# Placing the work between attention and the late expert tiles with a list scheduler instead of fixed steps

## The chip, the cores and the metric

The kernel runs on one core of a Trainium2 chip. A core has five engines with one instruction queue each, taken in order: PE (TensorE, matrix products), ACT (ScalarE), DVE (VectorE), POOL (GpSimd) and SP (SyncE, which here only starts DMA transfers). Engines wait for each other through semaphores; an instruction that waits holds up all that stands behind it on its engine. The metric is the time of one execution on the device in microseconds (us).

## What is computed

Decaying causal attention over 8 batches, 8 heads, 576 positions and head size 64, and behind it a mixture of 8 experts (512 to 1024 to 512) whose choice is sticky: a token keeps its predecessor's expert where its local gate is 0.5 or more.

```python
    scores = scale * np.matmul(q, k.transpose(0, 1, 3, 2))
    ...
    scores = np.where(causal, -1000000000.0, scores + decay)
    ...
    return np.matmul(attn, v).astype(np.float32)
...
    for b in range(B):
        prev_e = -1
        for s in range(S):
            fresh_e = int(np.argmax(logits[b, s]))
            if s == 0 or local_gate[b, s] < 0.5:
                e = fresh_e
            else:
                e = prev_e if prev_e >= 0 else fresh_e
            prev_e = e
            ...
            h = np.maximum(x[b, s] @ w1[e], 0.0)
            out[b, s] = p[e] * (h @ w2[e])
```

The 4608 tokens are x, the attention's output; logits and local gate are products of x with w_gate and w_local.

## The kernel before

Products of float32 values run as three float16 products (high by high, high by low, low by high), so each tensor is split into a high part (names that end in h) and a low part (names in l).

**Order of the phases.** Attention runs batch by batch. Routing (which token goes to which expert, in which place) follows in four groups of two batches, behind attention; the last group can only be routed when attention has ended. By then the first six batches are routed, and the first three tiles of 128 tokens of experts 0 and 1 come from them alone. These *early tiles* are computed right behind attention (L1703, L1725), and the last group's routing is done beside them. Then come the *late tiles* of expert 0 and of expert 1, then the six other experts, ranked by their number of tokens.

**One expert's early part.** `experts` (L1674) makes eight hidden tiles z of 128 columns, 12 products each (L1703, xT with wh and wl). For each, ACT writes hh (L1689) and then DVE hl (L1690), both from z in PSUM. z has two buffers, so tile n+2 waits for hl of tile n. Then three output tiles y follow, 24 products each (L1725, hh and hl with uh and ul); ACT scales y to o (L1694) and POOL scatters o to DRAM (L1695).

**Weights.** An expert's weights are eight blocks of 512 KB: four of w1 (to wh, wl) and four of w2 (to uh, ul). Each is loaded into a staging tile stg (L1857 and L1858; L1636 for the blocks split by POOL), then ACT casts the high part (L1845) and DVE makes the low part (L1849), or POOL does both (L1645, L326, L330). A staging tile comes free when its low part is made. Expert 0's w1 blocks are split by POOL during attention; its four w2 blocks, and all of expert 1's, are loaded behind attention, since expert 1's weights lie where attention's tiles were. `close_attention` gives that memory back; it stands behind the last batch's gate products (L837, from xt and xlt) and the sum that reads them (ACT half L844, DVE L848). Rank 0's weights are read ahead through the same staging tiles (`rank_loads`, L1863 and L1865).

**Routing of the last group.** `route` yields a chain over DVE, PE and ACT: maxima, `rows` (PE L1409, ACT kg L1414), a scan along 128 tokens (L1418), `ends` (PE L1422), `hold` (DVE crow L1435), `carries` (PE L1439), a second scan (L1446, copy so L1449), `back` (PE L1454), one-hot, prefix, `place` (PE L1479), slots, marks (L1505 to L1519), `invert` (PE L1525), and with it the indices (`all_idx`) by which POOL gathers the late tokens (L1671); SP transposes them (L1673). The results of a PE step share one PSUM bank, psG.

**What sets the order.** `run` (L1738) walks through the early experts' generator, which yields after every two products, and calls each piece of other work at a step number fixed in advance: AT for the gate and routing, RESTAT for the third group's probabilities, and `beside(step, ...)` for the rest. `experts` itself writes the hh and hl of a tile behind the next tile's products. An engine's instructions are thus queued in the order in which these calls come.

Of the kernel before, what the change touches and what calls it, by code (L numbers as in the profile page):

```python
# [9 lines left out]
F32 = mybir.dt.float32  # L10
# [18 lines left out]
CAP = 6  # L29
# [28 lines left out]
NP = 2  # L58
# [4 lines left out]
RESTAT = (0, 2, 8, 14, 20, 34, 35)  # L63
XG = 6
NP0 = 4
AT = (6, 15, 18, 30, 30, 36, 44, 49, 62)
# [9 lines left out]
def kernel(  # L76
# [1702 lines left out]
    for b in range(B):  # L1779
# [3 lines left out]
        for i, u in enumerate(units):  # L1783
# [85 lines left out]
    EX["NW"] = NW = []  # L1869

    def close_attention():
# [13 lines left out]
        NW.pop(0)()  # L1885
# [20 lines left out]
    def turn_xl():  # L1906
        (xl, xlt), ps = EX["xl"], bank()
        for i in range(4):
            nc.tensor.matmul(ps[:, 128 * i:128 * i + 128], lhsT=xl.rearrange("p a j d -> p (a j d)")[:, 128 * i:128 * i + 128],
                             rhs=ident16, start=(i == 0), stop=True, skip_group_check=True)  # L1910
        nc.vector.tensor_copy(flat(xlt), ps)

    crit, rest = route(B // 2 - 1, True)
    def both(*fs):
        return lambda: [whole(f) for f in fs]

    last = gate(B - 1)
# [4 lines left out]
    def beside(x, *fs):  # L1924

        at.append(x)
        todo.append(both(*fs))
# [66 lines left out]
    def half_tiles():  # L1994
# [14 lines left out]
        nc.sync.dma_start(out=T.hf[64:128], in_=T.hf[0:64])  # L2009
        NV.tensor_scalar(T.hfi, T.hf[:, 0], 2.0, T.hrow, ALU.mult, ALU.add)  # L2010
# [3 lines left out]
    def early(e, W, xT):  # L2014
        return experts(W, xT, EARLY, lambda t: EX["p"][:, CAP * e + t:CAP * e + t + 1],
                       lambda t: EX["s"][:, CAP * e + t:CAP * e + t + 1], ep, ep, 128 * EARLY, 2)
# [17 lines left out]
    def piece():  # L2034
        NW.pop(0)()
# [146 lines left out]
    for r in range(NR):  # L2182
# [99 lines left out]
```

## Time and profile before

| | us |
|---|---|
| median of 3 runs | 860.77 (857.41 to 861.67) |
| the profiled execution | 861.14 |
| its span, first to last instruction | 859.4 |
| mean granted TensorE clock | 0.963 |
| early part, first z to the first late z | 409.91 to 506.47 |

Busy time over the span: PE 91%, DVE 61%, ACT 51%, POOL 46%. The page's second part cuts the span into 40 slices of 21.5 us; a digit is the busy share in tenths. A row of the timeline gives start, duration, engine, line, operation, output and inputs, count, and in brackets the idle time before it with what ended it. PEclk is the granted clock: 1.00 is 2.4 GHz and 0.50 is 1.2 GHz.

### The profile page before, as it was taken

How to read it: one execution, taken by the hardware profiler on the slowest of the kernel's cores; microseconds unless marked ns; L12 is line 12 of the kernel's file. 1: busy time of each engine (PE TensorE's matmuls, PEld its weight loads, DVE VectorE, ACT ScalarE, POOL GpSimd, SP SyncE). 2: the span in 40 equal slices, each digit the busy share in tenths (PEclk: the TensorE clock that was granted, in tenths of full speed). 3: DMA queues.
4: the chain of work that ended last, by engine and by line, in shares of the span. 5: the costliest groups of instructions: out<-in, count | busy, mean ns of one | idle time of the engine just before them, and what ended most of it. 6: DMA issues, size and time to landing. Idle time of an engine off the chain costs nothing. (4 is left out here: it accounts for less than half of the span.)

```text
span 859.4 us, 21060 instructions
## 1 busy us (share of the span) xinstructions
PE 781.1 (91%) x8510; PEld 544.8 (63%) x8510; DVE 526.6 (61%) x1133; ACT 436.9 (51%) x811; POOL 391.3 (46%) x457
## 2 busy tenths in 40 slices
PE   5897999989999999979677899999999999999993
PEld 3675888768887788766333465674655758475541
DVE  8885888898989988987474524252470726333110
ACT  4785879678877788757222224242341414233210
POOL 9599839397948788446254013121303022120100
PEclk9897999999999999989799799999999999999997
DMA  6979949684868855477846512775372837544000
GB/s 167 180 163 186 201 97 186 136 182 116 172 153 158 175 106 110 114 142 148 214 160 162 181 37 90 182 184 174 125 215 69 211 120 185 163 139 124 26 26 22
DMA packets 196517, 122.46 MB, mean 142 GB/s; under 512 B 136220, under 2 KB 172318, under 8 KB 196396
## 3 DMA queue, kind: packets, MB, share of 16 engines
q1 hardware_dynamic: 190273, 101.68, 52.4%
q0 software_dynamic: 6144, 19.41, 7.1%
q8 instruction: 68, 1.11, 0.6%
q14 instruction: 32, 0.26, 0.1%
HBM read 72.41 MB, written 19.62 MB: 107 GB/s over the span
## 5 line engine op out<-in xcount | busy, mean ns | idle before, releaser
L1703 PE MATMUL z<-xT,wh 128*128 128x288 f16 (+4 forms) x960 | 186.2, 306 | 21.0 <-DVE hl L1690 21.0
L920 ACT ACTIVATE P<-st,nm 128x512 f32<-128x512 f32 (+3 forms) x288 | 153.0, 588 | 33.1 <-DVE nm L900 30.2
L1690 DVE SCALAR_TENSOR_TENSOR hl<-z,hh 128x576 f16<-128x576 f32 (+5 forms) x80 | 52.9, 662 | 178.6 <-ACT hh L1689 178.4
L900 DVE TENSOR_REDUCE nm<-st 128x1 f32<-128x512 f32 (+4 forms) x264 | 134.6, 544 | 17.7 <-PE st L896 13.5
L940 ACT CAST ph<-pt 128x512 f16<-128x512 f32 (+1 forms) x200 | 116.1, 584 | 46.8 <-PE pt L935 43.1
L1703 PEld LDWEIGHTS <-wh 128*128 128x128 f16 x960 | 94.0, 99 | 63.3 <-issue 21.9
L935 PE MATMUL pt<-ident,P 128*128 128x128 f32 x784 | 122.4, 280 | 6.4 <-DVE pl L944 5.6
L1695 POOL DMA_INDIRECT out_dram<-o,ranki x26 | 27.8, 1068 | 218.8 <-ACT o L1694 197.2
L1703 PE MATMUL z<-xT,wl 128*128 128x288 f16 (+4 forms) x480 | 120.5, 306 | 0.8 <-POOL wl L330 0.8
L944 DVE TENSOR_TENSOR pl<-pt,ph 128x512 f16<-128x512 f32 x168 | 111.6, 669 | 14.8 <-ACT ph L940 13.1
L1689 ACT ACTIVATE hh<-z 128x576 f16<-128x576 f32 (+5 forms) x80 | 45.9, 574 | 124.7 <-PE z L1703 124.6
L1725 PE MATMUL y<-ul,hh 128*128 128x512 f16 x288 | 109.2, 379 | 0.0
L1725 PE MATMUL y<-uh,hl 128*128 128x512 f16 x288 | 109.2, 379 | 0.0
L1725 PE MATMUL y<-uh,hh 128*128 128x512 f16 x288 | 109.2, 379 | 0.0
L935 PEld LDWEIGHTS pt<-ident,P 128*128 128x128 f32 x784 | 85.1, 143 | 23.0 <-issue 6.6
L1725 PEld LDWEIGHTS <-hh 128*128 128x128 f16 x576 | 56.2, 98 | 65.6
L914 PE MATMUL xp<-VH,pl 128*128 128x65 f16 (+1 forms) x960 | 92.1, 196 | 2.6 <-DVE pl L944 2.6
L914 PE MATMUL xp<-VH,ph 128*128 128x65 f16 (+1 forms) x960 | 93.8, 199 | 0.0
L914 PE MATMUL xp<-VL,ph 128*128 128x65 f16 (+1 forms) x960 | 92.7, 197 | 0.0
L914 PEld LDWEIGHTS <-ph 128*128 128x128 f16 (+1 forms) x1920 | 85.0, 104 | 6.4 <-issue 2.6
L889 PE MATMUL st<-KB,QB 70*128 70x256 f16 (+4 forms) x448 | 78.6, 283 | 7.5 <-DMA KB<-Ak 5.7
L889 PE MATMUL st<-Ak,Aq 128*128 128x256 f16 (+4 forms) x448 | 78.8, 286 | 4.5 <-ACT P L920 3.4
(375 smaller groups left out, 1305.7 us busy)
## 6 DMA issues: line engine op xcount, KB each, us to landing
stg<-in_moe_w_dram SPq DMA_DIRECT2D x64, 512.0 KB
xs<-xr SPq DMA_DIRECT2D x16, 512.0 KB
ldq<-in_q_dram SPq DMA_DIRECT2D x14, 512.0 KB
ldk<-in_k_dram SPq DMA_DIRECT2D x14, 512.0 KB
ldv<-in_v_dram SPq DMA_DIRECT2D x28, 256.0 KB
QB<-Aq SPq DMA_DIRECT2D x15, 256.0 KB
KB<-Ak SPq DMA_DIRECT2D x15, 256.0 KB
ldv<-in_v_dram SPq DMA_DIRECT2D x20, 64.0 KB
```

Source lines behind the costliest of these rows:

```text
L889: nc.tensor.matmul(st[p0:p0 + m, co:co + n], lhsT=queries(lq, kk, h, c), rhs=rhs, start=(ps == 0 and first and co == col), stop=(ps == 1), ...
L900: nc.vector.tensor_reduce(dst, src, axis=AX.X, op=ALU.max, negate=True)
L914: nc.tensor.matmul(xo, lhsT=a[:, c0:c0 + m], rhs=w[:, vi, :], start=False, stop=(i == n - 1 and jj == 2), skip_group_check=True)
L920: nc.scalar.activation(P[:, c0:c1].rearrange("p (k x r) -> p k r x", r=2, x=64), st[:, c0:c1].rearrange("p (k r x) -> p k r x", r=2, x=64) ...
L935: nc.tensor.matmul(U["pt"][:, i * 128:(i + 1) * 128], lhsT=P[:, i * 128:(i + 1) * 128], rhs=ident, is_transpose=True, start=(i == 0), stop ...
L940: nc.scalar.copy(U["ph"][:, :cols], U["pt"][:, :cols])
L944: nc.vector.tensor_tensor(U["pl"][:, :cols], U["pt"][:, :cols], U["ph"][:, :cols], ALU.subtract)
L1689: nc.scalar.activation(hv, z[:, 0:nh, 0:wd], AF.Relu)
L1690: nc.vector.scalar_tensor_tensor(lv, z[:, 0:nh, 0:wd], 0.0, hv, ALU.max, ALU.subtract)
L1695: nc.gpsimd.indirect_dma_start(out=outf, out_offset=bass.IndirectOffsetOnAxis(ap=scat(t), axis=0), in_=o, in_offset=None, bounds_check=NT ...
L1703: nc.tensor.matmul(z[:, a, 0:wd], lhsT=w[:, d, fc * 128:(fc + 1) * 128], rhs=xT[:, x, a * wd:(a + 1) * wd], start=(i == 0), stop=(i == len ...
L1725: nc.tensor.matmul(y, lhsT=a[:, fc, t * 128:(t + 1) * 128], rhs=u[:, fc], start=(i == 0), stop=(i == len(prods) - 1))
```

## The change

`flow` takes the place of `run` for the early part. The work is written as streams: the products of both experts, hidden high and low parts, outputs and scatters, the routing chain, the third group's probabilities, expert 0's w2 blocks, expert 1's blocks, two fetches of late tokens, the ranking, and the read-ahead for rank 0. Each step names its engine, an assumed cost, what it needs and what it gives. `flow` keeps a clock for each engine, takes the step that can start first (within 300 ns, on that engine, the stream with the lowest number), records it, and moves the clock on. It runs when the program is built, and only the order in which instructions are queued on each engine is its result. But for the drains below, the number of instructions, their sizes and the number of buffers stay as they were (SB is 3). The loads of expert 1's blocks from the third on are split off from `close_attention`, and late tokens are gathered and transposed in two streams. Besides, POOL gets a `drain` at the start of five ranked experts; in its queue each stands right behind the scatter of the expert before and ahead of the gathers for the next.

```diff
-RESTAT = (0, 2, 8, 14, 20, 34, 35)
...
-AT = (6, 15, 18, 30, 30, 36, 44, 49, 62)
+SB = 3
...
-                    stage = ctx.enter_context(tc.tile_pool(name="stage", bufs=3, side="right"))
+                    stage = ctx.enter_context(tc.tile_pool(name="stage", bufs=SB, side="right"))
...
-        NW.pop(0)()
+        NW_load.append(NW.pop(0))
...
-    def late_tok():
-        EX["x0"] = next_tokens(lambda i: EX["ga"][:, EARLY + i:EARLY + i + 1], CAP2[0] - 2 * EARLY)
...
-    todo = [turn_xl, lambda: whole(last[0]), both(*last[1:], close_attention, *crit[0:3]), both(*crit[3:6]), both(*crit[6:8]), both(*crit[8:10]),
-            both(*crit[10:13]), both(*crit[13:17]), both(*crit[17:19], all_idx, late_tok)]
-    at = list(AT)
...
-    def both_early():
-        yield from early(0, W0, EX["xT", 0])
-        yield from early(1, EX["W"], EX["xT", 1])
...
-    FW = static_weights(W0, 0, NP0, ha=HB)
-    FW.pop(0)()
-    for i in range(2 * (8 - NP0)):
-        beside(13 + 4 * i, lambda: FW.pop(0)())
-    for i in range(4 * NP):
-        beside(19 + 3 * i, lambda: EX["PW"].pop(0)())
-    REST = EX["rest"]
-    for x, f in zip(RESTAT, REST, strict=True):
-        beside(x, f)
-    beside(36, early_probs)
-    beside(19, open_ranks)
-    beside(64, lambda: EX.update(x1l=next_tokens(lambda i: EX["ga"][:, CAP + EARLY + i:CAP + EARLY + i + 1], CAP2[1] - 2 * EARLY)))
-    for i in range(16 - 2 * NP):
-        beside(65 + 24 * i // (16 - 2 * NP), piece)
-    for i, f in enumerate((totals, ranks, numbers, rank_loads, gathers, *rest, all_probs, scatters, half_tiles, caps)):
-        beside((63, 63, 64, 95, 96)[i] if i < 5 else 92 + 6 * (i - 5), f)
-    seq = sorted(range(len(at)), key=lambda x: at[x])
-    run(both_early(), [todo[x] for x in seq], [at[x] for x in seq], 400)
+    LAND = 2200
+    def flow(streams, t0):
+        clk = {x: t0 for x in ("PE", "ACT", "DVE", "POOL", "SP", "DMA")}
+        ev, lock = {}, {"owner": None, "free": (t0, "PE")}
+        heads = []
+        for prio, gen in streams:
+            heads.append([prio, gen, next(gen, None), (t0, None)])
+        while any(h[2] for h in heads):
+            able = []
+            for h in heads:
+                op = h[2]
+                if op is None or any(x not in ev for x in op.get("needs", ())):
+                    continue
+                if op.get("opens") and lock["owner"] is not None:
+                    continue
+                eng = op["eng"]
+                after = [ev[x] for x in op.get("needs", ())]
+                if op.get("seq", True) and h[3][1]:
+                    after.append(h[3])
+                if op.get("opens"):
+                    after.append(lock["free"])
+                t = max([clk.get(eng, t0), op.get("from", 0) + t0] + [e + (0 if src == eng else 200 if src != "SP" else 0) for e, src in after])
+                able.append((t, h[0], h))
+            first = min(able, key=lambda x: x[0])
+            t, _, h = min((x for x in able if x[2][2]["eng"] == first[2][2]["eng"] and x[0] <= first[0] + 300), key=lambda x: x[1])
+            op = h[2]
+            eng, cost = op["eng"], op.get("cost", 160)
+            if op.get("opens"):
+                lock["owner"] = h
+            op["fn"]()
+            if eng:
+                clk[eng] = t + cost
+            end = t + cost + op.get("lat", 0)
+            if "dma" in op:
+                clk["DMA"] = max(clk["DMA"], t + cost) + op["dma"]
+                end = clk["DMA"] + LAND
+            h[3] = (end, eng) if eng else h[3]
+            if op.get("shuts"):
+                lock.update(owner=None, free=(end, eng))
+            for x in op.get("gives", ()):
+                ev[x] = end, eng or "DVE"
+            h[2] = next(h[1], None)
...
+                    needs = [("hl", n - 2)] if c == 0 and n > 1 else []
+                    if fc == 0:
+                        needs += [("w", e, prods[c + 1][1])]
+                    yield op_("PE", 330, fn, needs, [("z", n)] if c + 2 == len(prods) else [])
...
+                    needs = [("hl", NF * e + fc)] if t == 0 else []
+                    if t == 0:
+                        needs += [("u", e, fc // 2)]
+                    if c == 0 and k > 1:
+                        needs += [("o", k - 2)]
+                    yield op_("PE", 432, fn, needs, [("y", k)] if c + 2 == len(prods) else [])
...
+            yield op_(("ACT", "DVE")[part], (500, 480)[part], fn, [("z", n)] if part == 0 else [("hh", n)], [(("hh", "hl")[part], n)])
...
+            if part == 0:
+                yield op_("ACT", 700, fn, [("y", k), "p", "closed"] + ([("sent", k - 4)] if k > 3 else []), [("o", k)])
+            else:
+                yield op_("POOL", 1000, fn, [("o", k)], [("sent", k)], lat=2500)
...
+            "slot": (("DVE", 170),) * 6, "marks": (("DVE", 640), ("DVE", 350), ("DVE", 250), ("DVE", 650), ("DVE", 760), ("DVE", 760)),
...
+        for i in range(n + half):
+            yield op_("POOL", 1050, lambda i=i: gather(i), needs, [(tag, i)], lat=2300)
+        for i in range(n + half):
+            yield op_("SP", 1300, lambda i=i: turn(i), [(tag, i)], [(tag, "t", i)], lat=2500, seq=False)
...
+    def blocks(pieces, first, ahead, give, needs=()):
+        load = lambda k: ("block", give, k)
+        yield op_("SP", 500 * ahead, pieces[0], needs, [load(k) for k in range(first, first + ahead)], dma=1600 * ahead)
+        for i in range(first, ND + NF // 2):
+            w = ("w", give, i) if i < ND else ("u", give, i - ND)
+            yield op_("ACT", 1060, pieces[1 + 2 * (i - first)], [load(i)], seq=False, gives=[("hi", give, i)])
+            more = i + ahead < ND + NF // 2
+            yield op_("DVE", 1220, pieces[2 + 2 * (i - first)], [("hi", give, i)], [w])
+            if more:
+                yield op_("SP", 0, nop, [w], [load(i + ahead)], dma=1600, seq=False)
...
+        yield op_("PE", 500, t1, opens=True, **{"from": 1000})
+        yield op_("DVE", 600, lambda: nc.vector.tensor_copy(flat(xlt), R["ps"]), shuts=True)
+        yield op_("PE", 450, last[0], opens=True, **{"from": 2800})
+        yield op_("PE", 700, last[1], **{"from": 4000})
+        yield op_("ACT", 360, last[2])
+        yield op_("DVE", 350, last[3], shuts=True)
+        yield op_(None, 0, close_attention, gives=["closed", "loads1"])
+        yield from steps_of(crit, {"marks": ["pinverted"]})
+        yield op_("DVE", 1200, all_idx, gives=["idx"])
...
+    def third():
+        yield op_("SP", 4000, rank_loads, ["numbers", ("u", 1, 3)])
...
+    def second():
+        yield op_(None, 0, nop, ["closed"])
+        PW = EX["PW"]
+        yield from by_pool(PW, 1)
+    def second_rest():
+        yield op_(None, 0, nop, ["closed", ("u", 0, 0)])
+        first = [lambda: NW_load[0]()] + list(NW)
+        yield from blocks(first, NP, ST + 3 - NP, 1)
+    FW = static_weights(W0, 0, NP0, ahead=SB, ha=HB)
+    ready = op_(None, 0, nop, gives=[("w", 0, d) for d in range(ND)])
+    e0 = CAP + EARLY
+    flow([(-9000, iter([ready])), (-3000, products()), (-6000, hidden(0)), (-6000, hidden(1)), (-4400, outputs(0)), (-4400, outputs(1)),
+          (-5600, routing()), (-5000, third_pair()), (-5500, blocks(FW, NP0, SB, 0)), (-300, second()), (-4400, second_rest()),
+          (-4400, fetch(CAP2[0] // 2 - EARLY, lambda i: EX["ga"][:, EARLY + i:EARLY + i + 1], "x0", ["idx"], bool(CAP2[0] % 2))),
+          (-4400, fetch((CAP2[1] - 2 * EARLY) // 2, lambda i: EX["ga"][:, e0 + i:e0 + i + 1], "x1l", [("x0", CAP2[0] // 2 - EARLY - 1)], bool(CAP2[1] % 2))),
+          (-3500, ranking()), (0, both_halves()), (-200, third())], clock["PE"])
...
         if r > 0:
+            todo.append(lambda: [nc.gpsimd.drain()])
+            at.append(2)
```

**ACT, right behind attention.** Names: hh is the high part of a hidden tile z of expert 0; uh from stg the cast of one w2 block of expert 0; half the gate; kg a routing step. Before:

```order
L1689 ACTIVATE hh_9640<-z_9642 128x384
L1845 ACTIVATE uh_8598<-stg_9634 128x1024
L1689 ACTIVATE hh_9640<-z_9658 128x384
L844 COPY half_9757<-psG_9704 128x36
L844 COPY half_9757<-psG_9704 64x9
L1845 ACTIVATE uh_8598<-stg_9636 128x1024
L1689 ACTIVATE hh_9640<-z_9686 128x384
L1845 ACTIVATE uh_8598<-stg_9638 128x1024
L1689 ACTIVATE hh_9640<-z_9730 128x384
```

The same place in the change:

```order
L2110 ACTIVATE hh_9687<-z_9642 128x384
L843 COPY half_9728<-psG_9669 128x36
L843 COPY half_9728<-psG_9669 64x9
L2110 ACTIVATE hh_9687<-z_9692 128x384
L2110 ACTIVATE hh_9687<-z_9742 128x384
L1844 ACTIVATE uh_8598<-stg_9636 128x1024
L1413 CAST kg_9827<-psG_9816 10x256
L2110 ACTIVATE hh_9687<-z_9795 128x384
L1844 ACTIVATE uh_8598<-stg_9638 128x1024
L1844 ACTIVATE uh_8598<-stg_9640 128x1024
L2110 ACTIVATE hh_9687<-z_9829 128x384
L2110 ACTIVATE hh_9687<-z_9872 128x384
```

The first cast of a w2 block stood between the first and the second hidden tile; now it stands behind the third, and the gate ahead of it. Three rows further on, uh from stg_9825 (expert 0's fourth w2 block) stands ahead of the last two hidden tiles.

**SP, in the middle of expert 0's early part.** Names: stg from w2 are blocks of expert 1; xT from xg are transposes of late tokens; eidi is the number of the rank 0 expert. Before, from expert 1's fifth block on:

```order
L1858 DMA stg_9794<-in_moe_w2_dram 128x2x512
L1858 DMA stg_9796<-in_moe_w2_dram 128x2x512
L1858 DMA stg_9798<-in_moe_w2_dram 128x2x512
L1673 DMA_TRANSPOSE xT_10049<-xg_10050 128x8x128
L1673 DMA_TRANSPOSE xT_10049<-xg_10053 128x8x128
L1673 DMA_TRANSPOSE xT_10067<-xg_10068 128x8x128
L1673 DMA_TRANSPOSE xT_10067<-xg_10071 128x8x128
L1673 DMA_TRANSPOSE xT_10067<-xg_10074 128x8x64
L1858 DMA stg_10088<-in_moe_w2_dram 128x2x512
L2026 TENSOR_LOAD eidi_9825
```

The same place in the change:

```order
L1857 DMA stg_9851<-in_moe_w2_dram 128x2x512
L1857 DMA stg_9853<-in_moe_w2_dram 128x2x512
L1857 DMA stg_9855<-in_moe_w2_dram 128x2x512
L1857 DMA stg_10024<-in_moe_w2_dram 128x2x512
L2170 DMA_TRANSPOSE xT_10063<-xg_10064 128x8x128
L2170 DMA_TRANSPOSE xT_10063<-xg_10113 128x8x128
L1999 TENSOR_LOAD eidi_10076
```

Expert 1's last block was loaded behind five transposes, which wait for the gathers; now it is loaded ahead of them. Three of the five transposes have moved behind rank 0's loads. Higher up in the same queue, the loads of expert 1's first two blocks have moved ahead of the load of expert 0's fourth w2 block.

## Rows read from the trace of the kernel before

**Rows 1.** The page, first and second part: PE's busy time, and its busy tenths in 40 slices of the span.

```profile
PE 781.1 (91%) x8510; PEld 544.8 (63%) x8510; DVE 526.6 (61%) x1133; ACT 436.9 (51%) x811; POOL 391.3 (46%) x457
...
PE   5897999989999999979677899999999999999993
```

**Rows 2.** Busy time by stretch: its ends, its length, busy us of PE, PEld, DVE, ACT and POOL, granted clock, DMA share, GB/s. First expert 0's and expert 1's early part, then three stretches at the lower clock.

```profile
409.90:463.20 53.30, 39.41 (x248) 20.36 (x244) 35.64 (x95) 14.87 (x24) 21.20 (x19) 0.87 0.58 166
463.20:506.40 43.20, 34.62 (x179) 17.92 (x178) 14.32 (x52) 7.08 (x13) 6.27 (x6) 0.88 0.51 156
425.30:430.30 5.00, 5.00 (x36) 2.61 (x35) 2.87 (x13) 2.52 (x5) 0.24 (x2) 0.50 0.64 203
437.20:440.40 3.20, 2.98 (x16) 1.73 (x14) 1.72 (x3) 0.49 (x1) 3.03 (x3) 0.50 0.31 81
475.85:481.30 5.45, 5.45 (x18) 2.51 (x18) 3.08 (x13) 0.65 (x2) 0.19 (x1) 0.50 1.00 321
```

**Rows 3.** What PE waited for: engine, line, what released it, us in total, times, longest. The first three rows are of 409.9 to 506.4, the last of 506.4 to 840.

```profile
PE z L1703 <- DVE hl L1690: 19.7, 6, 8.6
PE psG L1422 <- DVE crow L1429: 1.9, 1, 1.9
PE z L1703 <- POOL wl L330: 0.8, 1, 0.8
...
PE z L1703 <- DVE hl L1690: 1.3, 1, 1.3
```

**Rows 4.** PE in order of time: first early z, the products behind the four longest waits, first y of expert 0, first z of expert 1, first late z.

```profile
409.91 0.50 PE L1703 MATMUL z<-xT,wh 128*128 128x384 f16 x2
...
425.30 0.80 PE L1703 MATMUL z<-xT,wh 128*128 128x384 f16 x2 [7.13 <-DVE hl L1690]
...
435.90 0.16 PE L1422 MATMUL psG<-ident,sc 10*1 10x10 f16 x1 [1.90 <-DVE crow L1429]
...
444.87 0.50 PE L1703 MATMUL z<-xT,wh 128*128 128x384 f16 x2 [2.49 <-DVE hl L1690]
...
447.07 0.38 PE L1725 MATMUL y<-uh,hh 128*128 128x512 f16 x1
...
463.21 0.49 PE L1703 MATMUL z<-xT,wh 128*128 128x384 f16 x2
...
475.85 0.80 PE L1703 MATMUL z<-xT,wh 128*128 128x384 f16 x2 [8.58 <-DVE hl L1690]
...
506.47 0.38 PE L1703 MATMUL z<-xT,wh 128*128 128x256 f16 x2
```

**Rows 5.** ACT in order of time, ahead of the two longest waits of rows 4 and at expert 0's fourth w2 block; then DVE: the low part of the last batch's end (xl), its transposed copy (xlt), and the low parts ahead of the first long wait.

```profile
422.46 1.06 ACT L1845 ACTIVATE uh<-stg 128x1024 f16<-128x1024 f32 x1 [8.85 <-DMA stg<-in_moe_w_dram]
423.43 0.47 ACT L1689 ACTIVATE hh<-z 128x384 f16<-128x384 f32 x1
...
434.68 1.04 ACT L1845 ACTIVATE uh<-stg 128x1024 f16<-128x1024 f32 x1
...
472.87 1.06 ACT L1845 ACTIVATE uh<-stg 128x1024 f16<-128x1024 f32 x1 [8.77 <-DMA stg<-in_moe_w_dram]
...
411.20 0.43 DVE L288 TENSOR_TENSOR xl<-xnl,xl 128x256 f16<-128x256 f32 x1 [0.47 <-ACT xl L287]
...
413.62 0.69 DVE L1911 CAST xlt<-psG 128x512 f16<-128x512 f32 x1 [0.88 <-PE psG L1909]
...
423.55 1.23 DVE L1849 SCALAR_TENSOR_TENSOR ul<-stg,uh 128x1024 f16<-128x1024 f32 x1 [6.41 <-ACT uh L1845]
424.70 0.55 DVE L1690 SCALAR_TENSOR_TENSOR hl<-z,hh 128x384 f16<-128x384 f32 x1
```

**Rows 6.** SP's queue in order of time (a row of several counts the waits between them): expert 0's w2 loads, expert 1's first loads, the late tokens' transposes, expert 1's last load.

```profile
414.52 10.65 SPq L1858 DMA_DIRECT2D stg<-in_moe_w_dram  x4
427.77 0.82 SPq L1636 DMA_DIRECT2D stg<-in_moe_w_dram  x2
...
459.17 9.36 SPq L1673 DMA_TRANSPOSE xT<-xg  x5
468.62 0.53 SPq L1858 DMA_DIRECT2D stg<-in_moe_w_dram  x1
```

**Rows 7.** Busy time by stretch, columns as in rows 2: the landing of expert 0's first three w2 blocks, and that of the fourth.

```profile
422.00:424.00 2.00, 0.00 (x0) 0.00 (x0) 0.45 (x1) 1.43 (x2) 0.00 (x0) 0.50 0.94 360
...
426.00:428.00 2.00, 2.00 (x29) 1.44 (x28) 0.67 (x6) 0.93 (x3) 0.24 (x2) 0.50 0.71 251
```

**Rows 8.** DVE's first instruction of `marks` twice, in an earlier group with POOL at work and in the last group with POOL idle; and the first scan, with POOL at work on expert 1's first block.

```profile
365.23 1.22 DVE L1505 TENSOR_TENSOR HI<-imain,hm 128x480 f16<-128x480 f16 x1
...
450.06 0.66 DVE L1505 TENSOR_TENSOR HI<-imain,hm 128x480 f16<-128x480 f16 x1
...
434.43 1.42 DVE L1418 TENSOR_TENSOR_SCAN sc<-kg 10x128 f16<-10x128 f16 x1 [1.65 <-ACT kg L1414]
```

**Rows 9.** POOL in order of time: first gather of late tokens; then, among the ranked experts, the first and last gather that follow a last scatter, and the next expert's first scatter.

```profile
455.67 1.05 POOL L1671 DMA_INDIRECT xg<-xs,mg  x1 [13.02 <-DVE tot L1958]
...
609.48 1.00 POOL L1671 DMA_INDIRECT xg<-xs,ranki  x1 [0.31 <-issue]
...
614.57 0.91 POOL L1671 DMA_INDIRECT xg<-xs,ranki  x1 [0.30 <-issue]
639.46 1.43 POOL L1695 DMA_INDIRECT out_dram<-o,ranki  x1 [23.99 <-ACT o L1694]
```

More of the change, by code (lines that the diff above doesn't have):

```diff
@@ L1869 @@
     EX["NW"] = NW = []
+    NW_load = []
     def close_attention():
@@ L1904, in all_probs @@
         EX["pa"] = probs(invp, NM, "m", ktile)
[L1906 to L1911, printed above, removed]
     crit, rest = route(B // 2 - 1, True)
@@ L2009, in half_tiles, with half_rows @@
         nc.sync.dma_start(out=T.hf[64:128], in_=T.hf[0:64])
+    def half_rows():
         NV.tensor_scalar(T.hfi, T.hf[:, 0], 2.0, T.hrow, ALU.mult, ALU.add)
     assert all(RANK2[r] // 2 == RANK2[halves[0]] // 2 for r in halves) and halves == list(range(halves[0], halves[-1] + 1))
[L2014 to L2020 removed]
     eregs = {}
@@ new lines, in hidden, with fn @@
+    def hidden(part):
+        m = 128 * EARLY
+        for n in range(2 * NF):
+            def fn(n=n):
+                e, fc = divmod(n, NF)
+                if part == 0:
+                    if fc == 0:
+                        HID["hh", e] = ep.tile([128, NF, m], F16, name="hh")
+                        HID["hl", e] = ep.tile([128, NF, m], F16, name="hl")
+                    nc.scalar.activation(HID["hh", e][:, fc], HID["z", n][:, 0, 0:m], AF.Relu)
+                else:
+                    nc.vector.scalar_tensor_tensor(HID["hl", e][:, fc], HID["z", n][:, 0, 0:m], 0.0, HID["hh", e][:, fc], ALU.max, ALU.subtract)
+            yield op_(("ACT", "DVE")[part], (500, 480)[part], fn, [("z", n)] if part == 0 else [("hh", n)], [(("hh", "hl")[part], n)])
@@ new lines, in outputs, with fn @@
+    def outputs(part):
+        for k in range(2 * EARLY):
+            e, t = divmod(k, EARLY)
+            def fn(k=k, c=CAP * e + t):
+                if part == 0:
+                    HID["o", k] = EX["eo"].tile([128, DM], F32, name="o", bufs=4)
+                    nc.scalar.activation(HID["o", k], HID["y", k], AF.Copy, scale=EX["p"][:, c:c + 1])
+                else:
+                    nc.gpsimd.indirect_dma_start(out=outf, out_offset=bass.IndirectOffsetOnAxis(ap=EX["s"][:, c:c + 1], axis=0),
+                                                 in_=HID["o", k], in_offset=None, bounds_check=NT - 1, oob_is_err=False)
+            if part == 0:
+                yield op_("ACT", 700, fn, [("y", k), "p", "closed"] + ([("sent", k - 4)] if k > 3 else []), [("o", k)])
+            else:
+                yield op_("POOL", 1000, fn, [("o", k)], [("sent", k)], lat=2500)
@@ new lines, in steps_of, with fn @@
+    def steps_of(fs, needs={}, gives={}):
+        for f in fs:
+            nm = f.__name__
+            run, costs = {}, FLOW[nm]
+            for i, (eng, cost) in enumerate(costs):
+                last = i == len(costs) - 1
+                def fn(f=f, run=run, last=last):
+                    if not run:
+                        run["it"] = iter(f() or ())
+                    more = next(run["it"], StopIteration) is not StopIteration
+                    assert more != last, f.__name__
+                yield op_(eng, cost, fn, needs.get(nm, ()) if i == 0 else (), gives.get(nm, ()) if last else (),
+                          opens=nm in OPENS and i == 0, shuts=nm in SHUTS and last)
@@ new lines, in by_pool, with routing, t1 @@
+    def by_pool(pw, give):
+        for i in range(0, len(pw), 4):
+            for j in range(4):
+                last = j == 3
+                yield op_("POOL", 1150, pw[i + j], ["loads1"] if i + j == 0 else (), [("w", give, i // 4)] if last else ())
+    last = gate(B - 1)
+    def routing():
+        (xl, xlt), R = EX["xl"], {}
+        def t1():
+            R["ps"] = bank()
+            for i in range(4):
+                nc.tensor.matmul(R["ps"][:, 128 * i:128 * i + 128], lhsT=xl.rearrange("p a j d -> p (a j d)")[:, 128 * i:128 * i + 128],
+                                 rhs=ident16, start=(i == 0), stop=True, skip_group_check=True)
+        yield op_("PE", 500, t1, opens=True, **{"from": 1000})
[7 more added lines that the diff above has]
+        yield op_("DVE", 1200, all_idx, gives=["idx"])
@@ new lines, in ranking @@
+    def ranking():
+        yield op_(None, 0, open_ranks, ["idx"])
+        yield op_("PE", 60, totals, opens=True)
+        yield op_("DVE", 1050, ranks, shuts=True)
+        yield op_("DVE", 600, numbers, gives=["numbers"])
+        yield op_("DVE", 1100, gathers, gives=["gathers"])
+        yield from steps_of(rest)
+        yield op_("DVE", 620, all_probs)
+        yield op_("DVE", 1100, scatters)
+        yield op_("DVE", 1400, half_tiles, gives=["halves"])
+        yield op_("DVE", 1400, caps)
@@ new lines, in both_halves, with third_pair @@
+    def both_halves():
+        yield op_("SP", 500, nop, ["halves"], lat=16000)
+        yield op_("DVE", 120, half_rows)
+    def third():
+        yield op_("SP", 4000, rank_loads, ["numbers", ("u", 1, 3)])
+    def third_pair():
+        yield from steps_of(EX["rest"], gives={"pinvert2": ["pinverted"]})
+        yield op_("DVE", 560, early_probs, gives=["p"])
+    def second():
[6 more added lines that the diff above has]
+        yield from blocks(first, NP, ST + 3 - NP, 1)
```

61 lines of the change are left out of this document (55 added, 6 removed).

## The prediction

> **What bounds the kernel now.** I read the page's busy shares first. PE is busy 91% of the span, and in the 40 slices its digits are 9 or more nearly throughout, but for the start and slices 17 to 21 (some 365 to 470 us) [rows 1]. So the time is PE's, and only its holes can be won. Busy time by stretch puts them in the early part: PE works 39.41 of 53.30 us beside expert 0 and 34.62 of 43.20 us beside expert 1 [rows 2]; that is 22.5 us of idle time. PE's own waits there add up to the same, 19.7 + 1.9 + 0.8 = 22.4 us, while from 506.4 to 840 it waits 1.3 us in all [rows 3]. What is won ahead of 506 therefore comes off the end, if the late tiles find their inputs.
>
> The holes have a cost beside them. In three stretches (5.00, 2.98 and 5.45 us of work) the granted clock was 0.50, which is 1.2 GHz; each follows a wait, of 7.13, 1.90 and 8.58 us [rows 2, 4]. Half of that work, 6.7 us, is lost. At the full clock the early part's work is 39.41 + 34.62 - 6.7 = 67.3 us, and 67.3 + 22.4 + 6.7 gives back the 96.5 us between the first early z and the first late z [rows 4].
>
> The two long waits have one cause. ACT's queue held a cast of a w2 block ahead of a hidden tile's hh; the block landed only at 422.46 and 472.87, ACT had stood 8.85 and 8.77 us for it, and hh, ul and hl came behind [rows 5]. z has two buffers, so PE stopped.
>
> **The change part by part.** The work is the same; the order in the queues is new, so each wait is asked anew.
>
> First long wait (7.13 us, and 2.5 us of clock). The w2 loads keep their place on SP behind attention's last transfers, so uh starts at 422.46 as before [rows 5, 6]. But three hh now stand ahead of it, and their hl let PE go on to tile z4. A z tile takes 1.94 us: expert 1's 31.9 us at full clock, less 72 y products at 0.216 us (447.07 to 463.21 less 0.6 for L1525, by 72) and 0.8 us for L1576, by 8 [rows 2, 4]. In the new order, PE comes to 425.3 with z0 to z4, the gate and two routing steps; hl of z3, which z5 needs, is made behind uh and ul, at 422.46 + 1.06 + 1.23 + 0.5, some 425.3 as well. This wait goes.
>
> What is late next. (a) The turn of xl stands behind 4 products, at 410.6, and needs xl, ready at 411.63: 1.2 us with the semaphore. (b) The gate, now behind z0 (413.4), needs its bank, which xlt's copy frees no earlier than at 414.3: 1.2 us [rows 5]. (c) z6 needs hl of z4, which DVE queues behind two ul of 1.23 us, ready at 428.7; PE is there at 427.4: 1.5 us. (d) Three routing steps on PE wait for DVE's chain: crow 0.6, so 1.1, place 0.5. Together 6.1 us; the old waits at these places (0.8, 1.90, 2.49 and the small ones) are all in the 22.4.
>
> Second long wait (8.58 us and 2.7 us of clock). Expert 1's last block was loaded at 468.62, behind five transposes that waited for gathers from 455.67 on [rows 6, 9]. Now its load stands ahead of them and needs only a staging tile that POOL frees. The first loads for expert 1 wait for the gate, which ends near 418, not 427 (it stood behind the long wait), so they start some 9 us sooner than 427.77 [rows 6]. Expert 0's part shrinks to some 41 us, so expert 1 starts near 451; even at the old pace POOL's two blocks are split before that. I count this wait as gone.
>
> The moved transfers. The 53.30 and 43.20 us carried 166 and 156 GB/s, 15.6 MB [rows 2]; in 75 us that is 208 GB/s, and the trace moved 360 and 321 GB/s where weights alone came [rows 2, 7]. The late tokens' gathers have moved past scatters on POOL: the first two stand behind y0's and y1's, three behind y2's. Three transposes and rank 0's loads stand behind a number that DVE makes near 452. All are needed from some 485 on (expert 0's tokens) or 505 (the rest), so they are hidden by 20 to 30 us of products; without that cover a transpose costs its 2 us.
>
> The drains cost nothing on the path. Each stands between a last scatter and five gathers (609.48 to 615.5), behind which POOL idles 23.99 us until the next scatter at 639.46 [rows 9]. No row shows a drain: it lies between 0 and, if it waits for a scatter to land, a few us, all inside that idle time. I take 0.
>
> A cost the rows only bound. DVE's L1505 took 0.66 us with POOL idle and 1.22 us with POOL at work; the scan in the last group ran 1.42 us beside POOL's split [rows 8]. POOL's two blocks move to 427 to 438, beside other routing steps. If none of these is slowed it costs 0; if five us of them double, 5. The Trainium skill ("SBUF — State Buffer", section "SBUF: two separate sides") says that VectorE and GpSimd share a port pair as an exclusive lock, so that the one that starts second stands still rather than both running slower. By that rule a DVE step could wait for a whole POOL instruction each time; the trace agrees with a doubling at most, and shows no longer stop. I take 2.0 us for this and a stray stretch at the lower clock together, near the 1.5 us that the 2.98 us stretch cost [rows 2].
>
> Sum, against the profiled execution (861.14 us, span 859.4): 29.1 us of waits and clock go, 6.1 + 2.0 come: 21.0 less, **840 us**. That execution is 0.4 us above the median, which changes nothing.
>
> **The rivals.**
> A. *The wait moves to expert 0's fourth w2 block.* Its uh stands on ACT ahead of the last two hh, its ul on DVE ahead of so, for which PE waits in order; its load now follows two loads of expert 1. For: the same shape as the old stall. Against: after its issue at 425.2, 251 GB/s flowed from 426 to 428, one block [rows 6, 7], so 429 is likely. If it lands only at 434.68, where ACT took it up before [rows 5], so is ready at 439.2 and PE, at 433.9, waits 5.3 instead of 1.1 us and loses some 2.5 us of clock as after the 7.13: 6.7 more, **847 us**.
> B. *The second wait stays*, because expert 1's last blocks still come late: 8.6 + 2.7 us stay, **851 us**. Against: the order on SP.
> C. *Slower: many short waits keep the clock at 0.50.* The waits (a) to (d) stand close together; a wait of 1.90 us was followed by the lower clock, one of 2.49 us (444.87) by none at 450 [rows 2, 4]. If it holds through expert 0's whole part, its 35.4 us of full-clock work (67.3 - 31.9) cost as much again: 840 - 2 + 35, **873 us**. It decides the sign from 23 us of such work on; rows show 5.45 at most.
> D. *Nothing is won, because transfers set the pace*, not the order: if the 166 GB/s are all that the mix of transposes and loads can have, the early part keeps its length, **861 us**. Against: the rates above.
>
> **How the numbers follow.** Forecast 0.62 (836 to 844), A 0.18, B 0.06, D 0.08, C 0.06. About 0.5%, 4.3 us, is what a measurement of this kernel can tell from no change. Faster: forecast, A and B, 0.86; same: D, 0.08; slower: C, 0.06. The range goes from 833 (all 29.1 us gone is 832) to 850 (A with 3 us more), and leaves out B, C and D.
>
> **What would show it.** Right: expert 1's first z near 451 and the first late z near 485; PE's waits in the early part near 6 us in all, none over 2; clock near 1.00 there; no row of ACT standing 8 us for a block; PE without holes behind. Wrong: a wait of PE on so or crow of 4 us or more (A), ACT standing near the end of expert 0's part for the last block (B), a granted clock of 0.50 over ten us and more (C), or the first late z waiting for xT. Gathers of ranked experts that start more than 10 us later behind a drain would make its price wrong.

## The result and the profile after

The change runs in 829.22 us (827.57 to 830.46), the kernel before beside it in 861.22: ratio 0.9633 with the 95% interval 0.9596 to 0.967. Forecast were 840 us and a range of 833 to 850: the sign was right, the size 10.8 us short, the time outside the range.

The profiled execution spans 827.5 us, 31.9 less than before. First its early part by stretch (as [rows 2]: ends, length, busy us of PE, PEld, DVE, ACT, POOL, granted clock, DMA share, GB/s), up to expert 1's first z and up to the first late z:

```profile
408.50:450.20 41.70, 35.56 (x244) 18.94 (x242) 36.54 (x93) 16.15 (x25) 20.67 (x18) 1.00 0.70 216
450.20:482.40 32.20, 32.20 (x181) 17.27 (x180) 15.12 (x55) 6.26 (x12) 6.10 (x6) 1.00 0.73 205
```

41.70 and 32.20 us stand where 53.30 and 43.20 stood. The second stretch has no hole at all, and the clock is 1.00 throughout. PE in order of time (as [rows 4]), with every wait of over 0.2 us, and the first late z. Line numbers differ in the changed kernel: an early z is L2075, an early y L2090, an early hl L2112, a late z L1702.

```profile
408.51 0.56 PE L2075 MATMUL z<-xT,wh 128*128 128x384 f16 x2
...
409.82 0.28 PE L2203 MATMUL psG<-ident,xl 128*128 128x128 f16 x2 [0.43 <-ACT xl L286]
...
413.16 0.55 PE L836 MATMUL psG<-wg,xt 128*128 128x18 f16 x16 [1.30 <-DVE xlt L2207]
...
422.55 0.79 PE L1575 MATMUL psG<-rp,LO 128*128 128x144 f16 x10 [1.38 <-ACT kg L1413]
...
431.01 0.16 PE L1438 MATMUL psG<-ones,crow 1*10 1x1 f16 x1 [1.97 <-DVE crow L1434]
...
434.26 0.18 PE L1453 MATMUL psG<-idc,so 10*128 10x10 f16 x1 [0.27 <-DVE so L1448]
...
437.22 0.20 PE L1479 MATMUL psG<-EX,ones 128*128 128x80 f16 x1 [0.46 <-DVE EX L1472]
...
482.42 0.38 PE L1702 MATMUL z<-xT,wh 128*128 128x256 f16 x2
```

No wait reaches 2 us, where 7.13 and 8.58 us stood. With two of 0.17 and 0.15 us they sum to 6.1 us, and 67.76 us of work and 6.1 of waits are the 73.9 us of the early part. From the first late z to the end of the last scatter lie 340.2 us, in both kernels. But the end differs. POOL's last scatter, in the kernel before:

```profile
845.66 0.98 POOL L1695 DMA_INDIRECT out_dram<-o,ranki  x1 [4.20 <-ACT o L1694]
```

and in the changed one:

```profile
821.62 0.98 POOL L1694 DMA_INDIRECT out_dram<-o,ranki  x1 [4.20 <-ACT o L1693]
```

The span of before goes on for 12.76 us after this row (846.64 to 859.4), with no engine busy; that of the change for 4.90 (822.60 to 827.5). So the 31.9 us are 22.65 in the early part (96.56 to 73.91), 7.86 at the end, and 1.40 ahead of the early part (409.91 to 408.51), in attention, whose code is the same; in the profiles of the other runs the first early z lies between 407.9 and 412.1.

### The profile page after: what moved, and what is told of

It is laid out like the page before. It is cut to its first block, busy times and chain, and to the rows that moved or that the text cites. A ratio compares the mean times of both kernels' runs of the same rounds, so it can differ in the third digit from the quotient of the medians.

```text
span 827.5 us, 21063 instructions
## 1 busy us (share of the span) xinstructions
PE 774.9 (94%) x8510; PEld 542.8 (66%) x8510; DVE 526.9 (64%) x1133; ACT 437.8 (53%) x811; POOL 393.1 (48%) x457
## 5 line engine op out<-in xcount | busy, mean ns | idle before, releaser
L1689 DVE SCALAR_TENSOR_TENSOR hl<-z,hh 128x576 f16<-128x576 f32 (+4 forms) x64 | 44.2, 690 | 170.6 <-ACT hh L1688 170.4
L1702 PE MATMUL z<-xT,wh 128*128 128x288 f16 (+3 forms) x832 | 150.6, 297 | 1.3 <-DVE hl L1689 1.3
L1702 PEld LDWEIGHTS <-wh 128*128 128x128 f16 x832 | 81.0, 98 | 32.3 <-issue 2.2
L1702 PE MATMUL z<-xT,wl 128*128 128x288 f16 (+3 forms) x416 | 97.5, 297 | 0.0
L1688 ACT ACTIVATE hh<-z 128x576 f16<-128x576 f32 (+4 forms) x64 | 38.2, 597 | 100.8 <-PE z L1702 100.8
L1724 PE MATMUL y<-uh,hl 128*128 128x512 f16 x240 | 91.0, 379 | 0.0
L1724 PE MATMUL y<-ul,hh 128*128 128x512 f16 x240 | 91.0, 379 | 0.0
L1724 PE MATMUL y<-uh,hh 128*128 128x512 f16 x240 | 91.0, 379 | 0.0
L1724 PEld LDWEIGHTS <-hh 128*128 128x128 f16 x480 | 46.9, 98 | 54.9
```

The lines of the kernel that those rows point to most:

```text
L1688: nc.scalar.activation(hv, z[:, 0:nh, 0:wd], AF.Relu)
L1689: nc.vector.scalar_tensor_tensor(lv, z[:, 0:nh, 0:wd], 0.0, hv, ALU.max, ALU.subtract)
L1702: nc.tensor.matmul(z[:, a, 0:wd], lhsT=w[:, d, fc * 128:(fc + 1) * 128], rhs=xT[:, x, a * wd:(a + 1) * wd], start=(i == 0), stop=(i == len ...
L1724: nc.tensor.matmul(y, lhsT=a[:, fc, t * 128:(t + 1) * 128], rhs=u[:, fc], start=(i == 0), stop=(i == len(prods) - 1))
```

## The experiments

The runs of one group share their chip and its runs of the kernel before; the three groups were on three chips, so times of different groups are compared by their ratios to before.

**The end of the program: four runs.** The five drains alone put into the kernel before, at the place of the change; the change without them; with only the last one, as below; with only the first (r == 1 in its place).

```diff
-            todo.append(lambda: [nc.gpsimd.drain()])
-            at.append(2)
+            if r == NR - 1:
+                todo.append(lambda: [nc.gpsimd.drain()])
+                at.append(2)
```

> The kernel before with the five drains and nothing else. In the profile of before the span lasts 12.8 us beyond the end of the last scatter (846.64 to 859.4), in that of the change 4.9 us (822.60 to 827.5). Theory L (the end of the program must finish off on POOL every indirect DMA issued since the last drain, so drains ahead of the end shorten it): end 4.9 us, time 861.2 - 7.9 = 853.3 us, all else as before. Rival E (the end was shortened by the new order of the early part): end 12.8 us, time 861. Rival N (the drains cost time): above 861.

> The changed kernel without its five drains. Theory L: end 12.8 us behind the last scatter, time 829.2 + 7.9 = 837.1 us, early part as in the change (73.9 us from the first early z to the first late z). Rival E: end 4.9 us, 829 us. Rival N: below 829.

> The changed kernel with only the last of the five drains, that ahead of the last ranked expert's four scatters. Theory L (what counts is the number of indirect DMAs since the last drain, 4 here as in the change): end 4.9 us, 829 us. Rival F (each drain saves a fixed share, 7.9 / 5 = 1.6 us): end 12.8 - 1.6 = 11.2 us, 835.5 us.

> The changed kernel with only the first of the five drains. 43 of the 80 indirect DMAs stand behind it. Theory L, linear in the DMAs: 7.9 us by 76 (80 against 4) is 0.104 us each, so 43 - 4 = 39 cost 4.1 us more: end 9.0 us, 833 us. Rival F: end 11.2 us, 835.5 us. Rival A (any drain at all sets it right, as a start-up cost paid once): end 4.9 us, 829 us.

| kernel | median time, us | span beyond the last scatter, us (one profile each) | indirect DMAs behind the last drain |
|---|---|---|---|
| before (863.48 beside these) | | 12.76 (its first profile) | 80 |
| before with drains | 853.75, ratio 0.9874 (0.9839 to 0.991) | 5.01 | 4 |
| change without drains | 840.19, ratio 0.9723 (0.969 to 0.9755) | 12.68 | 80 |
| change, last drain only | 832.88, one execution | 5.12 | 4 |
| change, first drain only | 836.91, one execution | 8.88 | 43 |

The last scatter in these four runs, in the order of the table (their spans are 853.7, 838.4, 831.2 and 835.2 us):

```profile
847.71 0.98 POOL L1695 DMA_INDIRECT out_dram<-o,ranki  x1 [4.20 <-ACT o L1694]
...
824.74 0.98 POOL L1694 DMA_INDIRECT out_dram<-o,ranki  x1 [4.20 <-ACT o L1693]
...
825.10 0.98 POOL L1694 DMA_INDIRECT out_dram<-o,ranki  x1 [4.20 <-ACT o L1693]
...
825.34 0.98 POOL L1694 DMA_INDIRECT out_dram<-o,ranki  x1 [4.20 <-ACT o L1693]
```

That the drains shorten the end is shown both ways, by putting them in and by taking them out; E, N, F and A fall. Theory L's count fits: 80 against 4 indirect DMAs is 7.7 us, 0.10 us each, and by that the 43 should end at 9.0; they end at 8.88. The time gone since the last drain (or, without one, since the first indirect DMA) fits these four runs as well: some 41, 238 and 442 us for 5.0, 8.88 and 12.7. No run was made to part the two; those with one DMA left, in the last group, bear on it. Why the end takes that time, no row shows. One drain ahead of the last expert does the work of all five. (The first ratio leaves room for more than the end's 7.7 us; its interval begins at 7.8 us.) A drain has its own price. POOL's first gather behind a last scatter came 0.31 us after it in [rows 9]. In the changed kernel, behind the first and the second drain:

```profile
589.12 0.99 POOL L1670 DMA_INDIRECT xg<-xs,ranki  x1 [3.99 <-issue]
...
639.97 0.99 POOL L1670 DMA_INDIRECT xg<-xs,ranki  x1 [2.86 <-issue]
```

The gap grew by 3.7 us behind 37 DMAs and by 2.3 to 2.6 behind 10 (second to fourth drain; no gather follows the fifth). All of it lies in POOL's idle time, as the prediction had it.

**The early part: four runs.** Three put one of the two orders, or both, into the kernel before, at its fixed steps; the fourth takes one away from the change. The edit for ACT (expert 1's loads from the third block on had to move behind expert 0's fourth, as in the change), that for SP, and that in the changed kernel:

```diff
-        NW.pop(0)()
...
-        beside(13 + 4 * i, lambda: FW.pop(0)())
+        beside(25 + 3 * i, lambda: FW.pop(0)())
...
+    beside(29, piece)
...
-            both(*crit[10:13]), both(*crit[13:17]), both(*crit[17:19], all_idx, late_tok)]
+            both(*crit[10:13]), both(*crit[13:17]), both(*crit[17:19], all_idx)]
...
-    beside(64, lambda: EX.update(x1l=next_tokens(lambda i: EX["ga"][:, CAP + EARLY + i:CAP + EARLY + i + 1], CAP2[1] - 2 * EARLY)))
+    beside(89, late_tok)
+    beside(90, lambda: EX.update(x1l=next_tokens(lambda i: EX["ga"][:, CAP + EARLY + i:CAP + EARLY + i + 1], CAP2[1] - 2 * EARLY)))
...
-            yield op_("ACT", 1060, pieces[1 + 2 * (i - first)], [load(i)], seq=False, gives=[("hi", give, i)])
+            yield op_("ACT", 1060, pieces[1 + 2 * (i - first)], [("hh", 0)] if (give, i) == (0, first) else [load(i)], seq=False, gives=[("hi", give, i)])
```

> The kernel before, still at fixed steps, with expert 0's w2 casts put at later steps, so that three hh stand ahead of the first uh on ACT as in the change (expert 1's loads from the third block on move behind expert 0's fourth for it). Theory Q (the first long wait was the order on ACT alone): the 7.13 us and some 2.5 us of clock behind it go, short waits of up to 3 us may come: 852 to 855 us; the second wait of 8.6 us stays. Rival W (the wait only moves on, to the next block or the y products): 859 us or more.

> The kernel before, at fixed steps, with the late tokens' gathers and transposes issued behind expert 1's last weight load. Theory Q (the second long wait was that load standing behind five transposes on SP): 8.58 + 2.7 us go, 850 to 853 us, the first wait of 7.1 us stays, no wait for xT at the late tiles. Rival W (the block comes late anyway, or the late tiles wait for their tokens): 857 us or more.

> Both edits of the two runs before together, in the kernel before at fixed steps, without drains. Theory Q: the two orders are what the change won in its early part, so the time comes near that of the change without drains: 861.2 - 9.6 - 11.3 = 840 us, up to 843 with new short waits. Rival S (the list scheduler's other placings carry a good part): 846 us or more.

> The changed kernel with one step altered: the first cast of expert 0's w2 stands on ACT behind the first hh again, ahead of the second. Theory Q: hh of z1 waits for the block's landing (about 421 us), PE stops for z2 some 4 us and runs a few us at the lower clock behind it: 834 to 838 us. Rival P (the other placings take the stop in): 829 to 831 us.

Beside 862.94 us for before, the ACT order alone took 857.42 (ratio 0.9935, 0.9915 to 0.9956), the SP order alone 852.07 (0.9896, 0.9862 to 0.993), both 846.30 (0.9819, 0.9783 to 0.9854); the change with uh first took 838.66 (0.9738, 0.9705 to 0.9771).

The SP order by itself wins 9.0 us by the ratio (6.0 to 11.9), where theory Q said 11.3: expert 1 has no wait left, and the late tiles none for xT. The ACT order wins 5.6 us, not 9.6: rival W has part of it. PE, in the run with both orders:

```profile
425.10 0.50 PE L1703 MATMUL z<-xT,wh 128*128 128x384 f16 x2 [2.46 <-DVE hl L1690]
...
439.22 0.82 PE L1703 MATMUL z<-xT,wh 128*128 128x384 f16 x2 [4.18 <-DVE hl L1690]
```

The 7.13 us shrank to 2.46, and 4.18 came at the last z tile, with the clock at 0.50 for 5 us behind it. DVE in the same run shows why: hl stood behind a low part of w2 that took 2.19 us, and this behind steps of routing and probabilities. Below it stand two rows of POOL, which splits an expert 1 block beside them.

```profile
434.43 0.89 DVE L1449 COPY so<-sc 10x128 f16<-10x128 f16 x1
...
435.43 0.96 DVE L1618 SCALAR_TENSOR_TENSOR xp<-xp,invp 128x9 f32<-128x9 f32 x1
...
436.50 2.19 DVE L1849 SCALAR_TENSOR_TENSOR ul<-stg,uh 128x1024 f16<-128x1024 f32 x1
438.62 0.55 DVE L1690 SCALAR_TENSOR_TENSOR hl<-z,hh 128x384 f16<-128x384 f32 x1
...
435.33 1.05 POOL L326 TENSOR_SCALAR wh<-stg 128x1024 f16<-128x1024 f32 x1
436.46 3.25 POOL L330 TENSOR_TENSOR wl<-stg,wh 128x512 f16<-128x512 f32 x2
```

Three of these DVE steps are longer than with POOL idle: so took 0.89 us for 0.21, xp 0.96 for 0.17 and ul 2.19 for 1.22. That is 2.4 us of the 4.18, and it comes from POOL's work at that moment, which the third group of runs takes up.

So rival S holds for a part: both orders win 15.6 us by the ratio, the change without drains 23.9. What lies between them must come from the other placings of the scheduler; no run takes one of these by itself. Seen from the change, uh put ahead of the second hh brings the old stop back:

```profile
425.05 0.80 PE L2075 MATMUL z<-xT,wh 128*128 128x384 f16 x2 [7.16 <-DVE hl L2112]
```

That wait was forecast too small (4 us): on DVE, ul and four small steps stood ahead of hl as well, and the gate's copy stood on ACT behind uh. By the ratios (0.9738 less the 0.9640 that the change has in the next group, of 862.94) the step costs some 8.5 us, so P falls; the clock was 0.50 from 425.05 to 430.5, which is 2.7 us of it.

**The change again, and three tries at more.** The change itself; kg ahead of the first uh, with a drain behind each of the last expert's first three scatters; expert 1's first two w1 loads behind its next four, so that POOL splits them later; all of these.

```diff
-        yield from steps_of(crit, {"marks": ["pinverted"]})
+        yield from steps_of(crit, {"marks": ["pinverted"]}, {"rows2": ["kg"]})
...
-            yield op_("ACT", 1060, pieces[1 + 2 * (i - first)], [load(i)], seq=False, gives=[("hi", give, i)])
+            yield op_("ACT", 1060, pieces[1 + 2 * (i - first)], [load(i)] + ["kg"] * ((give, i) == (0, first)), seq=False, gives=[("hi", give, i)])
...
             for f in after:
                 f()
+                if dr:
+                    nc.gpsimd.drain()
...
-        for _, f in first[0:2]:
-            f()
+        EX["PL"] = [f for _, f in first[0:2]]
...
-        yield op_(None, 0, close_attention, gives=["closed", "loads1"])
+        yield op_(None, 0, close_attention, gives=["closed"])
...
-        first = [lambda: NW_load[0]()] + list(NW)
+        yield op_("SP", 0, lambda: [f() for f in NW_load + EX["PL"]], ["closed", ("u", 0, 0)], ["loads1"])
+        first = [nop] + list(NW)
```

> The changed kernel itself, to stand on the same chip as the three runs beside it. All theories: ratio to before 0.963 as in its first comparison, end 4.9 to 5.1 us behind the last scatter. Its early part was 73.9 us there, with PE's waits for kg 1.38 and for crow 1.97 us and no stretch at the lower clock; the same code without drains showed 75.7 us on another chip, with 2.40 for kg and a stretch at the lower clock behind the 1.97: between 73.9 and 76 us expected.

> Two edits at two ends of the changed kernel. First: expert 0's first w2 cast needs kg in the planner's terms, so ACT has the routing step kg ahead of it and not behind. Theory K (kg's late read of psG is again a small step standing behind a cast whose block has not landed): PE's wait for kg, 1.4 to 2.4 us, is gone, early part 1.4 to 2.4 us shorter. Rival M (the cast put later makes hl or the y products late): a new wait of PE on hl or uh of the same size, no gain. Second: POOL is drained behind each of the last expert's first three scatters too, so one indirect DMA instead of four is left for the end. Theory L: 3 x 0.104 = 0.3 us less, end 4.6 to 4.8 us. Rival: end unchanged or longer.

> The changed kernel with expert 1's first two w1 loads behind its next four on SP and no other instruction moved, so that POOL splits these blocks some 8 us later, after the scans of the last group's routing. Theory X (DVE steps stand still while a POOL instruction runs): hold, crow, so, OHA and IN, which took 0.67, 1.08, 0.88, 0.69 and 1.16 us beside POOL's split, take 0.16, 0.16, 0.21, 0.24 and 0.32 as in earlier groups with POOL idle; PE's wait for crow falls from 1.97 us to under 1. Expert 1's first z may wait up to 2 us for its blocks. Rival Y (they are slow for another reason, such as reading PSUM): durations and the 1.97 stay.

> The three edits of the two runs before together. If each holds by itself: 2 to 4 us less than the changed kernel. If expert 1's blocks come too late once the rest is shorter, PE waits for wh or wl at expert 1's first z and the gain is under 1 us.

Beside 862.60 us, they took 831.35 (ratio 0.9640, 0.9614 to 0.9666), 834.63 (0.9672, 0.9644 to 0.9699), 835.71 (0.9695, 0.9666 to 0.9723) and 836.62 (0.9699, 0.9671 to 0.9727). None beats the change.

The end behaved as theory L has it: 5.02 us with 4 DMAs left, 4.56 and 4.75 with one. By the count it should be 4.7, by the time since the last drain, here 5 us for some 41, 4.3: the count fits better, on two profiles. In the second run kg's wait, 3.09 us in the change on this chip, is gone, but the planner, told of one more need, placed the routing steps earlier in PE's queue: `invert` stands behind 18 y products of expert 0 instead of 36, and PE waited there for LO.

```profile
441.07 0.39 PE L1524 MATMUL psG<-RH,LO 128*128 128x96 f16 x5 [2.95 <-DVE LO L1518]
```

The early part grew from 76.2 to 79.4 us: 1.0 us of it in PE's waits and 2.3 in its work (71.5 for 69.3 us), which ran at 0.50 for some 3.5 us twice, where the change beside it has one such stretch. So K names that wait rightly, and its removal was given back.

The third run left every queue but SP's as it was. Five DVE steps, in the change of the first profile, with POOL at work on the split:

```profile
429.18 0.67 DVE L1432 TENSOR_SCALAR hold<-ends 1x10 f32<-1x10 f32 x1
429.88 1.08 DVE L1434 TENSOR_TENSOR_SCAN crow<-hold,ends 1x10 f16<-1x10 f32 x1
...
433.32 0.88 DVE L1448 COPY so<-sc 10x128 f16<-10x128 f16 x1
...
434.78 0.69 DVE L1459 TENSOR_TENSOR OHA<-code,iexp 128x80 f16<-128x80 f32 x1
435.50 1.16 DVE L1468 TENSOR_TENSOR_SCAN IN<-carry,OHA 128x80 f16<-128x80 f16 x1
...
428.67 2.27 POOL L329 TENSOR_TENSOR wl<-stg,wh 128x512 f16<-128x512 f32 x2
431.01 1.98 POOL L1644 TENSOR_SCALAR stg<-stg 128x1024 f32<-128x1024 f32 x1
433.07 1.06 POOL L325 TENSOR_SCALAR wh<-stg 128x1024 f16<-128x1024 f32 x1
434.21 2.27 POOL L329 TENSOR_TENSOR wl<-stg,wh 128x512 f16<-128x512 f32 x2
```

and in this run, with POOL idle until 436.54:

```profile
428.75 0.16 DVE L1432 TENSOR_SCALAR hold<-ends 1x10 f32<-1x10 f32 x1
428.94 0.17 DVE L1434 TENSOR_TENSOR_SCAN crow<-hold,ends 1x10 f16<-1x10 f32 x1
...
431.62 0.21 DVE L1448 COPY so<-sc 10x128 f16<-10x128 f16 x1
...
433.09 0.24 DVE L1459 TENSOR_TENSOR OHA<-code,iexp 128x80 f16<-128x80 f32 x1
433.36 0.32 DVE L1468 TENSOR_TENSOR_SCAN IN<-carry,OHA 128x80 f16<-128x80 f16 x1
```

4.48 us became 1.10, and PE's wait for crow went: theory X holds. The rows of POOL show the stop itself: crow ended 0.02 us, so 0.07 and IN 0.18 us behind the end of the POOL row that it overlaps, however short the step is by itself. (POOL's step at 431.01, begun while DVE's next ul ran, took 1.98 us where it takes 1.04 alone, so the stop goes both ways.) The kernel did not gain, since the split then met the next steps. Two LO of 1.55 us together took 3.46, and PE, which had no such wait in the change, waited 1.39 and 1.31 us for them:

```profile
441.33 0.39 PE L1524 MATMUL psG<-RH,LO 128*128 128x96 f16 x5 [1.39 <-DVE LO L1518]
...
443.02 0.39 PE L1524 MATMUL psG<-RH,LO 128*128 128x96 f16 x5 [1.31 <-DVE LO L1518]
```

Its early part took 77.7 us against 76.2 of the change beside it, which is the difference of the profiled spans (831.2 and 829.6); what made the other executions longer still, 4.4 us between the medians, stays open. All three edits together kept PE waiting 1.91 us for expert 1's wh, as feared.

## Why the prediction was right and where it failed

**The step that failed is the drains.** The prediction said that they "cost nothing on the path" and took 0, with bounds of 0 and a few us, both of cost. They gain 7.9 us, all at the end of the span. That a drain hides in POOL's idle time was right; what was never asked is what work it takes over, and from where. The trace of before held the answer: 12.76 us between its last scatter and its end, with nothing running. The prediction counted the span's end as given and read no row of it. With this term the same sum gives 832 us, within 0.4% of what was measured in either group (829.22 and 831.35). Of the 10.9 us by which the spans moved more than forecast, 7.9 are this; 1.6 lie in the early part, and 1.4 in attention, whose code is the same.

**Both long waits** went as told, and with them the clock's loss behind them. First late z: 482.42, forecast near 485; expert 1's first z: 450.66, forecast near 451. The early part was to shrink by 21.0 us; it did by 22.65 here, and to 76.2 us on the chip of the last group, where 75.5 had been forecast. The cause of the second wait is shown by the SP order alone, that of the first by uh put back; but in the kernel before the ACT order alone leaves 2.46 of the 7.13 us and brings the 4.18.

**What is late next** came out right as a sum, 6.1 us forecast and measured, by luck: gate (1.30 for 1.2) and place (0.46 for 0.5) were right, the turn of xl (0.60 for 1.2), z6 (0.15 for 1.5) and so (0.27 for 1.1) too dear, crow (1.97 for 0.6) too cheap, and kg (1.38) was missed: it stood on ACT behind the same uh whose landing had caused the first wait.

```profile
421.19 1.06 ACT L1844 ACTIVATE uh<-stg 128x1024 f16<-128x1024 f32 x1 [2.20 <-DMA stg<-in_moe_w_dram]
422.15 0.34 ACT L1413 CAST kg<-psG 10x256 f16<-10x256 f32 x1
```

**The cost that the rows only bound** was mis-read. The prediction held that DVE beside POOL is slowed to "a doubling at most", and said that the trace shows no longer stop. crow took 1.08 us for 0.17, more than six times as long; POOL's halves of a split took 1.13 us. So the rule of the Trainium skill ("SBUF — State Buffer", section "SBUF: two separate sides"), that the one that starts second stands still, fits these rows, and a doubling does not. The reading had rested on one pair of rows (0.66 and 1.22 us), where a stop of half a microsecond looks like a factor; the scan of 1.42 us beside it [rows 8] takes 0.40 in the change with POOL idle. And the trace of before had a longer stop: its so beside POOL, where the fastest of the same step there takes 0.21 us.

```profile
440.26 2.38 POOL L330 TENSOR_TENSOR wl<-stg,wh 128x512 f16<-128x512 f32 x2
...
441.73 1.00 DVE L1449 COPY so<-sc 10x128 f16<-10x128 f16 x1
```

The 2.0 us set aside for this and a stray stretch at the lower clock have no place of their own in the first profile: the clock held, and the slowed steps are part of crow's 1.97 us above. In the last group's profile of the change a stretch at the lower clock did come, and PE's work took 69.3 us for 67.8.

**The rivals.** A did not come in the change, where ACT's wait for the fourth block was 1.55 us and no PE wait followed; a wait of its size came in the run with both orders, from DVE's queue. B and D fell with the two stretches in the result: no wait of expert 1 is left, and the early part moved 216 and 205 GB/s. C fell too: in none of the five profiles of the change, with or without drains, does a stretch at the lower clock in the early part last over 4 us.

## What to carry to other kernels

Read the stretch between the last instruction and the end of the span like any other: here 12.8 us lay there, and one drain of the queue of indirect DMAs, put where its engine idles, took 7.6 of them (12.68 to 5.12). A change with no visible gain has to be asked what it takes over from another place, and its bounds go below nothing unless a row excludes it. And before one step is moved out of another's way, look at what stands where it will land, on DVE and POOL together: three tries at the waits that were left only moved them.

## What the runs showed of the hardware that was not expected

The end of the program grew by 0.10 us for every indirect DMA that POOL had issued since its last drain (4.56 and 4.75 us with 1, 4.9 to 5.2 with 4, 8.88 with 43, 12.7 to 12.9 with 80).

Beside POOL's split of a weight block, a DVE step of 0.17 us took up to 1.08 us and ended with the POOL instruction; with POOL idle the same five steps took 1.10 us for 4.48. In the last group's profile of the change, crow fell between two POOL instructions and took 0.17 us, so where the two engines meet differs from one execution to the next.

The same wait is followed by different clocks. Stretches ahead of and behind the 1.97 us wait for crow, columns as above, in the changed kernel's profile:

```profile
429.00:431.00 2.00, 0.05 (x1) 0.00 (x0) 1.93 (x6) 1.05 (x1) 1.93 (x2) 1.00 1.00 387
431.00:435.00 4.00, 3.71 (x22) 1.98 (x23) 3.81 (x8) 1.90 (x3) 3.82 (x3) 1.00 0.90 318
```

and in the change without drains, whose queues are the same up to there:

```profile
431.00:433.00 2.00, 0.03 (x2) 0.01 (x1) 1.93 (x6) 0.61 (x1) 1.92 (x3) 1.00 0.98 376
433.00:437.00 4.00, 4.00 (x15) 2.05 (x16) 3.03 (x5) 0.49 (x1) 3.83 (x3) 0.57 0.79 283
```

After the same wait the first stays at 2.4 GHz, and the second works for most of 4 us at 1.2 GHz. Some 8 us ahead, PE had waited 1.38 us for kg in the first and 2.40 us in the second; what decides it stays open.
